# A table of pieces for units 2 to 13 of an attention and FFN kernel, and two three-operand weight passes on VectorE

## The chip, the cores and the metric

One NeuronCore of a Trainium2 chip runs the whole program in one launch. The metric is the device time in microseconds (us); a time stands for the median of several runs, and beside it stands one execution that the hardware profiler recorded.

## The reference

```python
# q, k, v: [4, 8, 576, 64]; w1: [1, 32]; b1: [32]; w2: [32, 8]
scores = (1/8) * q @ k.T                         # per batch and head
x = log1p(|i - j|) / log1p(max(i, 1))            # i, j: positions
bias = relu(x[..., None] @ w1 + b1) @ w2         # one 576x576 table per head
attn = softmax(scores + bias, over j)
y = attn @ v                                     # heads put side by side: [2304, 512]
h = y @ w_in                                     # w_in: [512, 2048], w_out: [2048, 512]
out = (h * cos(h)) @ w_out                       # float32
```

The inputs `moe_w_in` and `moe_w_out` come as 64-bit floats; the kernel reads them as pairs of 32-bit words and makes a high and a low float32r part of each itself.

## The kernel before

**Bias (0 to some 65 us).** 36 groups of rows of the bias tables are computed and stored to DRAM (`sc`), and read back as tiles `bt`.

**Attention (some 65 to 284 us).** The 16 units are pairs of heads of one batch. A unit has five slots, one for each tile of query rows; slot `j` has tile `tiles[j]` of `[0, 1, 4, 2, 3]`. Tiles 0 to 3 have 128 rows for each of two heads; tile 4 (slot 2) holds the last 64 rows of both heads, and counts as one head. For a tile the steps are, with short names that the text uses:

- S (`qk`, from the change on `scores`, L418): the scores, 12 matmuls (6 for tile 4) on TensorE into the PSUM tiles `s` (tag "s", two of them, two banks each). The array is used as two row tiles of 64x128, one per head; for tile 4 as one of 128x128.
- M (L431): VectorE adds the bias, keeps the row minimum of the negated sum, and frees `s`. One for each head.
- E (L449): ScalarE takes the exponential and the row sum. One for each head.
- D and R (L462, L465): VectorE adds 1e-9 to each head's sum and takes the reciprocal.
- N (L472): POOL multiplies the tile with it. One for each head.
- T (`halves`, L479): TensorE transposes the tile three slots later, in 64x128 row tiles, into the two PSUM banks `pm` (one buffer each). It also transposes pieces of neighbouring tiles into the bank `pt`.
- A and B (`keep_main`): ScalarE (A, L507) and VectorE (B, L510) copy the two halves of `pm` to `PT`, and so free `pm`. L (`keep_left`) copies `pt`.
- V (`pv`, L547): attn @ v for half `hf` (0: tiles 0, 1; 1: tiles 4, 2, 3), in five chunks of 128 keys, in column tiles of 128x64, into the one PSUM bank `pv`. One chunk is four matmul records. K (`keep_x`, L507 `xT`): ScalarE copies the finished half to `xT` and frees the bank.
- For the unit after next, q and k are transposed into a PSUM tile of tag "s" (F, `spare`), copied out by C (k: VectorE, q: ScalarE) and X (last rows), and split by POOL into high and low parts (P, `split`, L185 and L189).

**Weights.** A weight part is loaded as `raw`, made absolute by ScalarE ("abs", L93) and goes through four VectorE passes of 128x512 in `widen_w` (steps 0, 0.5, 1, 2: L101, L103, L105, L107; here W0, W0.5, W1, W2), a ScalarE copy (step 3) and a POOL subtraction (step 4, L111). Eight of the 32 parts are widened in the attention stage, one every two units, 24 in the FFN.

**FFN (some 284 us to the end).** 96 steps; each has 12 matmuls into `ph` (`ffn1`, L733), the cosine gate (L737, L743, L744, L748, L752, L756, L762), and 9 matmuls into `po` (`ffn2`, L779). `ph` has two buffers, and `gate` (L752, VectorE) frees one. POOL splits `xT` into `xs` (L532, L533), VectorE adds `po` up (L803).

**Order.** Every engine runs its instructions in the order in which the Python code issues them. In the attention stage `slot(i)` issues slot `i = 5u + j` by hand: S and M, then E of the last tile, T of the tile of three slots before, V, the copies, D, R, splits, N, loads, and the weight steps of `W_PLAN` and its kin. TensorE's order in a unit is thus

S0, T2, V(0: 0, 1), S1, V(0: 2, 3, 4), T3, F, S2, T4, S3, T0, V(1: 0, 1, 2), S4, T1, V(1: 3, 4)

with the number of the slot of the tile behind S and T, and half and chunks behind V.

Of the kernel before, what the change touches and what calls it, by code (L numbers as in the profile page):

```python
# [28 lines left out]
def kernel(  # L29
# [66 lines left out]
    def widen_w(fc, part, step=None):  # L96
        r, t, b = raw[fc, part], W[fc], wabs[fc, part]
        lo, hi = r[:, :, 0], r[:, :, 1]
        u = b.bitcast(U32)
        if step in (None, 0):  # L100
            nc.vector.tensor_scalar(b, b, 2.0**-15, None, ALU.max)  # L101
        if step in (None, 0.5):
            nc.vector.tensor_scalar(u, u, 3, 0x3FFFFFF8, ALU.logical_shift_left, ALU.bitwise_and)  # L103
        if step in (None, 1):
            nc.vector.scalar_tensor_tensor(u, lo, 29, u, ALU.logical_shift_right, ALU.bitwise_or)  # L105
        if step in (None, 2):
            nc.vector.scalar_tensor_tensor(u, hi, 0xC0000000, u, ALU.bitwise_and, ALU.bitwise_or)  # L107
        if step in (None, 3):
            nc.scalar.activation(out=t[:, 0, part], in_=b, func=AF.Copy)  # L109
        if step in (None, 4):  # L110
            nc.gpsimd.tensor_tensor(t[:, 1, part], b, f(t[:, 0, part]), ALU.subtract)  # L111

    with tc.manual_schedule():
# [82 lines left out]
        def natural(u, x):  # L196
            return nat[u, "k" if x == "x" else x].rearrange("p r h d -> p r (h d)")
# [13 lines left out]
            else:  # L211
                nc.scalar.activation(out=o, in_=i, func=AF.Copy, scale=-0.125)

        def keep_turned(u, x, ps):
            if x == "x":
                pq, pk_ = (ps[:, 0:64], ps[:, 64:128]) if not isinstance(ps, list) else ps
                o = kt.rearrange("p (a x) -> p a x", x=64)[:, 0:10:9]
                i = pk_.unsqueeze(1).to_broadcast([128, 2, 64])
                if u == 1:
# [6 lines left out]
                if u > 1:  # L226
# [179 lines left out]

        cur = {}

        def qk(u, j):
            t = tiles[j]  # L410
            heads = range(2 if t < 4 else 1)
            s = [ps_s.tile([128, 2, 512], F32, tag="s", name="s") for h in heads]
# [13 lines left out]
            hp = units[u][0]  # L426
            P[u, j] = pp.tile([128, 1152], F32, tag="p", name="P")
            for h in heads:
                neg = P[u, j][:, 576 * h : 576 * h + 576]
                m = sv.tile([128, 2], F32, tag=f"m{h}", name="m")  # L430
                nc.vector.tensor_tensor_reduce(  # L431
                    neg.rearrange("p (a x) -> p a x", a=2),
                    s[h][:, :, 0:HALF],
                    bias[hp, t, h].rearrange("p (a x) -> p a x", a=2),
                    1.0,
                    3.0e38,
                    ALU.add,
                    ALU.min,
                    m[:, 0:1],
                )  # L440
                cur[u, j, h] = (neg, m)

        P, dn, rc = {}, {}, {}

# [10 lines left out]
                accum_out=dn[u, j][:, h : h + 1],  # L455
            )

        def recip(u, j, step):
            n = 2 if tiles[j] < 4 else 1
            if step == 0:  # L460
                for h in range(n):
                    nc.vector.tensor_scalar(dn[u, j][:, h : h + 1], dn[u, j][:, h : h + 1], 1e-9, None, ALU.add)  # L462
            else:
                rc[u, j] = sv.tile([128, 2], F32, tag="rc", name="rc")
                nc.vector.reciprocal(rc[u, j][:, 0:n], dn[u, j][:, 0:n])  # L465
# [67 lines left out]
            nc.gpsimd.tensor_tensor(l, src, f(h), ALU.subtract)  # L533
            X[g, n, c] = (h, l)

        X_ = {}

        def pv(u, hf, chunks):
            hp, b = units[u]
            n = vN[u % 2]  # L540
# [15 lines left out]

        def keep_x(u, hf):
            hp, b = units[u]
# [13 lines left out]
        W_EARLY = [("abs", -1)]  # L572
        W_MID = [(3, 9)]
        W_PLAN = [(0, 2), (0.5, 3), (1, 7), (2, 8), ("load", 8), (4, 12)]
        get = lambda i: jobs[i] if 0 <= i < len(jobs) else None

        shared = {}
# [2 lines left out]
        def weights(i, plan):  # L580
            for step, at in plan:
                w, r = divmod(i - at, 10)
                if r == 0 and 0 <= w < len(wparts):
                    if step == "load":
                        if w + 2 < len(wparts):
                            load_w(*wparts[w + 2])
                    elif step == "abs":
                        abs_w(*wparts[w])
                    else:
                        widen_w(*wparts[w], step)  # L590

        def slot(i):
# [88 lines left out]
            if now and u == 0 and j == 0:  # L681
                split(1, "k")
            elif now and u == 0 and j == 1:
                split(1, "q")
            elif now:
                for du, x, step in POOL_PLAN[j]:
                    if u + du < NU and not (u == 0 and x == "q"):
# [6 lines left out]
            if now:  # L694
                if i == 1:
                    load(0, "v")
                for du, x in LOAD_PLAN[j]:
                    if u + du < NU:
# [232 lines left out]
```

## Time and profile before

| | |
|---|---|
| median of 3 runs | 699.49 us (697.37 to 701.4) |
| the profiled execution | 700.05 us |
| its span, first to last instruction | 698.3 us |
| mean granted TensorE clock | 0.995 of full speed |
| busy in the span: TensorE, VectorE, ScalarE, POOL | 98%, 83%, 62%, 58% |

Matmuls are pipelined and their ends are modelled, so two records overlap and a busy TensorE tells little: what counts is the distance from the start of one block of matmuls to the start of the next. In the rows below a line merges neighbouring instructions of one form; "PEld" are weight loads, "L431" is line 431 of the kernel.

### The profile page before, as it was taken

How to read it: one execution, taken by the hardware profiler on the slowest of the kernel's cores; microseconds unless marked ns; L12 is line 12 of the kernel's file. 1: busy time of each engine (PE TensorE's matmuls, PEld its weight loads, DVE VectorE, ACT ScalarE, POOL GpSimd, SP SyncE). 2: the span in 40 equal slices, each digit the busy share in tenths (PEclk: the TensorE clock that was granted, in tenths of full speed). 3: DMA queues.
4: the chain of work that ended last, by engine and by line, in shares of the span. 5: the costliest groups of instructions: out<-in, count | busy, mean ns of one | idle time of the engine just before them, and what ended most of it. 6: DMA issues, size and time to landing. Idle time of an engine off the chain costs nothing.

```text
span 698.3 us, 15617 instructions
## 1 busy us (share of the span) xinstructions
PE 683.7 (98%) x5747; PEld 564.9 (81%) x5747; DVE 581.1 (83%) x1342; ACT 434.9 (62%) x935; POOL 403.2 (58%) x486
## 2 busy tenths in 40 slices
PE   6998999999999999999999999999999999999997
PEld 3576777777777777788989999889989888999986
DVE  7997888888898888667887888999998998976666
ACT  5896888889888887645565554544545445433342
POOL 0306898988989899745454463563653744753300
PEclk9998999999999999999999999999999999999999
DMA  7798348238435501001121010111110111011112
GB/s 208 254 334 238 86 104 207 67 96 219 104 83 148 157 19 49 31 4 57 31 59 34 31 61 31 33 58 31 60 31 31 60 31 32 0 46 46 46 46 92
DMA packets 84446, 58.57 MB, mean 84 GB/s; under 512 B 62225, under 2 KB 70801, under 8 KB 84369
## 3 DMA queue, kind: packets, MB, share of 16 engines
q1 hardware_dynamic: 83024, 56.88, 28.2%
q8 instruction: 46, 0.75, 0.5%
q10 hardware_dynamic: 1344, 0.69, 0.4%
q14 instruction: 32, 0.25, 0.1%
HBM read 41.94 MB, written 15.61 MB: 82 GB/s over the span
## 4 chain that ended last, share of the span: by engine, by line
PE 94%; DVE 2%; DMA 1%; issue 1%; SPq 0%; ACT 0%; DVEq 0%; ACTq 0%
PE ph L733 29%; PE po L779 29%; PE pv L547 12%; PE s L418 11%; PE pm L479 6%; PE pa L332 5%; PE spare L479 1%; PE pt L479 1%; DVE P L431 1%; DVE ht L317 1%; DMA lt<-in_ltab_dram 1%; DMA bt<-sc 0%; DMA nk<-in_q_dram 0%; DVE acc L803 0%; DVE edge L302 0%
## 5 line engine op out<-in xcount | busy, mean ns | idle before, releaser
L431 DVE CUSTOM_DVE_ANT_0 P<-s,bt 128x576 f32<-128x576 f32 x144 | 103.7, 753 | 23.9 <-PE s L418 23.9
L472 POOL TENSOR_SCALAR P<-P,rc 128x576 f32<-128x576 f32 x144 | 107.7, 759 | 24.9 <-DVE rc L465 11.1
L737 ACT ACTIVATE a<-ph,quarter 128x384 int32<-128x384 f32 x96 | 55.6, 579 | 102.2 <-PE ph L733 101.2
L533 POOL TENSOR_TENSOR xs<-xT,xs 128x384 fp32r<-128x384 f32 x96 | 107.7, 1122 | 8.0
L449 ACT ACTIVATE P<-P,m 128x576 f32<-128x576 f32 x144 | 110.0, 768 | 1.0 <-POOL P L472 0.8
L733 PE MATMUL ph<-xs,wpre 128*128 128x384 f32 x576 | 109.4, 338 | 0.0
L733 PE MATMUL ph<-xs,w 128*128 128x384 f32 x576 | 108.3, 337 | 0.0
L743 DVE SCALAR_TENSOR_TENSOR r<-a,ph 128x384 f32<-128x384 int32 x96 | 52.8, 550 | 65.5 <-ACT a L737 65.3
L733 PEld LDWEIGHTS ph<-xs,wpre 128*128 128x128 f32 x576 | 101.8, 188 | 5.3 <-DVE a L752 0.9
L733 PEld LDWEIGHTS ph<-xs,w 128*128 128x128 f32 x576 | 101.5, 188 | 4.7 <-DVE a L752 0.6
L748 ACT ACTIVATE r<-r,hpi 128x384 f32<-128x384 f32 x96 | 59.3, 617 | 72.9 <-DVE r L744 72.7
L418 PE MATMUL s<-kN,qT 64*128 64x288 f32 (+1 forms) x864 | 93.8, 315 | 2.0 <-DVE m L431 1.5
L418 PEld LDWEIGHTS s<-kN,qT 64*128 64x128 f32 (+1 forms) x864 | 72.2, 188 | 27.1 <-DVE dn L462 8.5
L532 POOL TENSOR_SCALAR xs<-xT 128x384 fp32r<-128x384 f32 x96 | 62.7, 653 | 38.8 <-PE ph L733 38.8
L547 PE MATMUL pv<-PT,vN 128*64 128x320 f32 (+1 forms) x512 | 76.4, 420 | 0.0
L762 DVE TENSOR_TENSOR gl<-a,gh 128x384 fp32r<-128x384 f32 x96 | 74.4, 775 | 2.0 <-ACT gh L756 2.0
L779 PE MATMUL po<-wpre,gh 128*128 128x512 f32 x288 | 75.3, 397 | 0.0
L779 PE MATMUL po<-w,gh 128*128 128x512 f32 x288 | 75.2, 395 | 0.0
L111 POOL TENSOR_TENSOR w<-wb,w 128x512 fp32r<-128x512 f32 x16 | 20.7, 1296 | 89.3 <-ACT w L109 89.3
L744 DVE SCALAR_TENSOR_TENSOR r<-a,r 128x384 f32<-128x384 int32 x96 | 60.5, 630 | 3.3
L756 ACT ACTIVATE gh<-a 128x384 fp32r<-128x384 f32 x96 | 49.8, 519 | 21.2 <-DVE a L752 21.2
L779 PEld LDWEIGHTS po<-wpre,gh 128*128 128x128 f32 x288 | 53.4, 188 | 9.4 <-issue 0.5
(97 smaller groups left out, 1175.8 us busy)
## 6 DMA issues: line engine op xcount, KB each, us to landing
sc<-rt SPq DMA_DIRECT2D x36, 295.5 KB, 4.4
raw<-in_moe_w_in_dram SPq DMA_DIRECT2D x16, 512.0 KB, 3.8
raw<-in_moe_w_out_dram SPq DMA_DIRECT2D x16, 512.0 KB, 3.5
bt<-sc SPq DMA_DIRECT2D x16, 288.0 KB, 3.6
out_dram<-acc SPq DMA_DIRECT2D x17, 256.0 KB, 2.0
nk<-in_k_dram SPq DMA_DIRECT2D x32, 128.0 KB, 3.4
bt<-sc SPq DMA_DIRECT2D x16, 256.0 KB, 4.3
vN<-in_v_dram SPq DMA_DIRECT2D x32, 128.0 KB, 2.9
```

Source lines behind the costliest of these rows:

```text
L418: nc.tensor.matmul(s[h][:, hf, 0:HALF], qTs[u % 2][r, a, 128 * t : 128 * t + 128] if t < 4 else qTs[u % 2][:, a, 512:640], kN[u][r, b, o : ...
L431: nc.vector.tensor_tensor_reduce(neg.rearrange("p (a x) -> p a x", a=2), s[h][:, :, 0:HALF], bias[hp, t, h].rearrange("p (a x) -> p a x", ...
L449: nc.scalar.activation(out=P[u, j][:, 576 * h : 576 * h + 576], in_=neg, func=AF.Exp, bias=m[:, 0:1], scale=-1.0, accum_out=dn[u, j][:, h ...
L472: nc.gpsimd.tensor_scalar(p, p, r, 1.0, ALU.mult, ALU.mult)
L532: nc.gpsimd.tensor_scalar(h, src, 1.0, 1.0, ALU.mult, ALU.mult)
L533: nc.gpsimd.tensor_tensor(l, src, f(h), ALU.subtract)
L547: nc.tensor.matmul(ps[64 * h : 64 * h + 64, 0 : WQ[hf]], a, m, start=(c == 0), stop=(c == 4), tile_position=(0, 64 * h), skip_group_check= ...
L733: nc.tensor.matmul(ps, a, x, start=(i == 0), stop=(i == 3 * KD - 1))
L744: nc.vector.scalar_tensor_tensor(r, n, -TWO_PI_LO, r, ALU.mult, ALU.add)
L748: nc.scalar.activation(out=r, in_=r, func=AF.Sin, scale=SIN_SCALE, bias=hpi)
L762: nc.vector.tensor_tensor(gl, a, f(G[key][0]), ALU.subtract)
L779: nc.tensor.matmul(O[n][i], a[:, 128 * i : 128 * i + 128], w, start=(i0 == 0 and p == 0), stop=(i0 == GF - 1 and p == 2),)
```

## The change

`slot` no longer writes out slots 10 to 69 (units 2 to 13). They come from a table `PLAN` of five rows, one for each slot of a unit; an entry is a piece, its due slot counted from the start of the unit (or part of weights) that it belongs to, and its arguments. Units 0, 1, 14 and 15 keep the old order; `caught_up` issues, at the two borders, what one order has done and the other not. V's chunks are spread anew, so that TensorE's order in a unit is

S0, T2, V(0: 0, 3, 1), S1, T3, V(0: 2), F, S2, V(0: 4), T4, S3, T0, V(1: 0, 1, 2), S4, T1, V(1: 3, 4)

On VectorE the order of a unit is M0 (head 0), D4, M0 (head 1), X, R4, B2; M1, M1, D0, R0; B3, C, M2, D1, R1, B4; M3, M3, D2, R2, B0; M4 (head 0), D3, M4 (head 1), B1, R3. W1 stands first in slot 0 and W2 first in slot 3, of odd units (3, 5, ... 13), W0 last in slot 3 of odd units, W0.5 last in slot 2 of even units. On ScalarE, K of the second half stands behind both E of slot 4, no longer ahead of them. D takes its heads as an argument (both, in this table). Steps 0 and 0.5 of `widen_w`, in attention and FFN alike, become three-operand instructions: step 0 has its own input as second tensor, step 0.5 a constant column broadcast along the row.

```diff
+    field = const.tile([128, 1], F32, name="field")
@@ widen_w
         if step in (None, 0):
-            nc.vector.tensor_scalar(b, b, 2.0**-15, None, ALU.max)
+            nc.vector.scalar_tensor_tensor(b, b, 2.0**-15, b, ALU.max, ALU.max)
         if step in (None, 0.5):
-            nc.vector.tensor_scalar(u, u, 3, 0x3FFFFFF8, ALU.logical_shift_left, ALU.bitwise_and)
+            nc.vector.scalar_tensor_tensor(
+                u, u, 3, field[:, 0:1].bitcast(U32).to_broadcast([128, 512]), ALU.logical_shift_left, ALU.bitwise_and
+            )
...
+        nc.vector.memset(field, 2.0 - 2.0**-20)
...
-        def qk(u, j):
+        def scores(u, j):
...
+        def lowest(u, j, heads):
...
-        def recip(u, j, step):
+        def recip(u, j, step, heads=(0, 1)):
             n = 2 if tiles[j] < 4 else 1
             if step == 0:
-                for h in range(n):
+                for h in [h for h in heads if h < n]:
...
+        PLAN = [
+            [('W', 5, 1), ('E', 5, 4, 0), ('E', 5, 4, 1), ('S', 0), ('M', 0, 0, 0), ('D', 5, 4), ('K', 10, 1), ('T', 5, 2), ('M', 0, 0, 1), ('X', -10, 'k'), ('W', 10, 3), ('P', -5, 'q', 2), ('V', 5, 0, 0), ('X', -10, 'q'), ('LB', 0, 0), ('R', 5, 4), ('N', 5, 4, 0), ('V', 5, 0, 3), ('W', 10, 'load'), ('N', 5, 4, 1), ('L', 5, 0), ('W', 10, 4), ('A', 5, 2), ('B', 5, 2), ('V', 5, 0, 1)],
+            [('S', 1), ('W', -4, 'abs'), ('E', 1, 0, 0), ('E', 1, 0, 1), ('M', 1, 1, 0), ('M', 1, 1, 1), ('D', 1, 0), ('LB', 1, 1), ('R', 1, 0), ('N', 1, 0, 0), ('T', 6, 3), ('N', 1, 0, 1)],
+            [('A', 7, 3), ('B', 7, 3), ('V', 7, 0, 2), ('F', -8, 'k'), ('E', 2, 1, 0), ('E', 2, 1, 1), ('F', -8, 'q'), ('S', 2), ('C', -8, 'k'), ('P', -3, 'q', 1), ('M', 2, 2, 0), ('V', 7, 0, 4), ('LD', -13, 'q'), ('D', 2, 1), ('C', -8, 'q'), ('R', 2, 1), ('N', 2, 1, 0), ('K', 7, 0), ('N', 2, 1, 1), ('T', 7, 4), ('B', 7, 4), ('A', 7, 4), ('W', 2, 0.5), ('LB', 2, 2)],
+            [('S', 3), ('LD', -12, 'k'), ('E', 3, 2, 0), ('W', 8, 2), ('M', 3, 3, 0), ('T', 3, 0), ('M', 3, 3, 1), ('D', 3, 2), ('R', 3, 2), ('V', 8, 1, 0), ('B', 3, 0), ('N', 3, 2, 0), ('W', -2, 0), ('A', 3, 0), ('V', 8, 1, 1), ('LB', 3, 3), ('L', 8, 1), ('P', -7, 'k', 0)],
+            [('V', 9, 1, 2), ('E', 4, 3, 0), ('S', 4), ('M', 4, 4, 0), ('T', 4, 1), ('P', -6, 'q', 0), ('E', 4, 3, 1), ('D', 4, 3), ('P', -6, 'k', 1), ('A', 4, 1), ('V', 9, 1, 3), ('M', 4, 4, 1), ('V', 9, 1, 4), ('LD', -1, 'v'), ('B', 4, 1), ('LB', 4, 4), ('P', -6, 'k', 2), ('R', 4, 3), ('N', 4, 3, 1), ('N', 4, 3, 0)],
+        ]
...
+        def planned(i):
+            for op, f, *a in PLAN[i % 5]:
+                if op == "W":
+                    weights(i, [(a[0], f)])
+                elif 0 <= (i - f) // 5 < NU:
+                    step(op, (i - f) // 5, i, f, a)
+
+        FIRST, LAST = 10, 5 * (NU - 2)
...
         def slot(i):
             u, j = divmod(i, 5)
+            if i in (FIRST, LAST):
+                caught_up(i)
+            if FIRST <= i < LAST:
+                return planned(i)
```

## Rows read from the trace of the kernel before

**Rows 1.** The page: shares of the span, by engine, in the chain that ended last

```profile
PE 94%; DVE 2%; DMA 1%; issue 1%; SPq 0%; ACT 0%; DVEq 0%; ACTq 0%
```

**Rows 2.** Windows: one unit; length, then busy us of PE, PEld, DVE, ACT, POOL

```profile
178.77:193.06 14.29, 14.29 (x196) 10.63 (x195) 12.48 (x43) 11.73 (x32) 13.05 (x18) 1.00 0.38 85
```

**Rows 3.** Timeline, TensorE in one unit: start us, length us, what

```profile
183.37 1.05 PE L418 MATMUL s<-kN,qT 64*128 64x288 f32 x12
...
184.27 0.22 PE L479 MATMUL pm<-ident,nk 64*128 64x64 f32 x2
...
184.85 1.08 PE L547 MATMUL pv<-PT,vN 128*64 128x256 f32 x8
...
185.86 1.16 PE L418 MATMUL s<-kN,qT 64*128 64x288 f32 x12
...
186.95 1.08 PE L547 MATMUL pv<-PT,vN 128*64 128x256 f32 x8
...
187.87 0.60 PE L547 MATMUL pv<-PX,vN 128*64 128x256 f32 x4
...
188.40 0.71 PE L479 MATMUL pm<-ident,P 64*128 64x64 f32 x16
...
188.95 0.41 PE L479 MATMUL spare<-ident,nk 64*128 64x64 f32 x8
...
189.20 0.42 PE L479 MATMUL spare<-ident,nq 64*128 64x64 f32 x8
...
189.54 1.06 PE L418 MATMUL s<-kN,qT 128*128 128x288 f32 x6
...
190.53 0.65 PE L479 MATMUL pm<-ident,P 64*128 64x64 f32 x14
...
191.18 1.33 PE L418 MATMUL s<-kN,qT 64*128 64x288 f32 x12
...
192.23 0.77 PE L479 MATMUL pm<-ident,P 64*128 64x64 f32 x16
...
193.06 1.30 PE L547 MATMUL pv<-PT,vN 128*64 128x320 f32 x8
```

**Rows 4.** Timeline of the same unit: ScalarE, VectorE and POOL, with idle time before

```profile
183.51 0.44 ACT L507 ACTIVATE xT<-pv 128x320 f32<-128x320 f32 x1 [0.67 <-PE pv L547]
...
183.72 0.88 POOL L189 TENSOR_TENSOR kN<-kt,kN 128x320 fp32r<-128x320 f32 x1
183.85 0.77 ACT L449 ACTIVATE P<-P,m 128x576 f32<-128x576 f32 x1
...
184.46 0.76 DVE L431 CUSTOM_DVE_ANT_0 P<-s,bt 128x576 f32<-128x576 f32 x1 [0.59 <-PE s L418]
...
185.15 0.75 DVE L431 CUSTOM_DVE_ANT_0 P<-s,bt 128x576 f32<-128x576 f32 x1
...
191.45 0.68 DVE L510 COPY PT<-pm 128x512 f32<-128x512 f32 x1
```

**Rows 5.** By line: three weight passes; least, median and longest ns of one

```profile
L101 DVE TENSOR_SCALAR wb<-wb x32: 404/728/1232, 62.0 to 595.0; 128x512 f32<-128x512 f32 x32
...
L103 DVE TENSOR_SCALAR wb<-wb x32: 426/1114/1179, 65.0 to 595.8; 128x512 uint32<-128x512 uint32 x32
...
L105 DVE SCALAR_TENSOR_TENSOR wb<-raw,wb x32: 669/684/1506, 77.7 to 599.5; 128x512 uint32<-128x512 uint32 x32
```

**Rows 6.** Timeline, FFN stage: weight passes, and what stands beside and behind them

```profile
346.58 1.20 POOL L533 TENSOR_TENSOR xs<-xT,xs 128x384 fp32r<-128x384 f32 x1
346.83 1.50 DVE L105 SCALAR_TENSOR_TENSOR wb<-raw,wb 128x512 uint32<-128x512 uint32 x1
...
457.27 1.12 DVE L103 TENSOR_SCALAR wb<-wb 128x512 uint32<-128x512 uint32 x1
458.31 0.54 DVE L752 TENSOR_TENSOR a<-r,ph 128x384 f32<-128x384 f32 x1
...
458.91 2.37 PE L733 MATMUL ph<-xs,w 128*128 128x384 f32 x12
```

More of the change, by code (lines that the diff above doesn't have):

```diff
@@ L212, in keep_pair, with keep_turned @@
                 nc.scalar.activation(out=o, in_=i, func=AF.Copy, scale=-0.125)
-        def keep_turned(u, x, ps):
+        def keep_turned(u, x, ps, part=None):
             if x == "x":
@@ L218, in keep_turned @@
                 i = pk_.unsqueeze(1).to_broadcast([128, 2, 64])
+                if part == "k":
+                    nc.vector.tensor_copy(o, i)
+                    return
                 if u == 1:
@@ L225, in keep_turned @@
                     )
-                if u > 1:
+                if u > 1 and part is None:
                     nc.vector.tensor_copy(o, i)
@@ L407, with scores_of_rest, scores_of_rest_begun @@
         cur = {}
-        def qk(u, j):
+        def scores_of_rest(u, s, step):
+            for n, (a, b) in enumerate(((0, 0), (0, 1), (1, 0))):
+                for h in range(2):
+                    r, hf = slice(64 * h, 64 * h + 64), h ^ step
+                    o = HALF * hf + 64
+                    nc.tensor.matmul(
+                        s[:, hf, 0:HALF],
+                        qTs[u % 2][r, a, 512:640],
+                        kN[u][r, b, o : o + HALF],
+                        start=(step == 0 and n == 0),
+                        stop=(step == 1 and n == 2),
+                        tile_position=(r.start, 0),
+                    )
+        live = {}
+        def scores_of_rest_begun(u):
+            live[u, 2] = [ps_s.tile([128, 2, 512], F32, tag="s", name="s")]
+            scores_of_rest(u, live[u, 2][0], 0)
+            nc.sync.keepalive_nop(ins=[nc.sync.lower_ap(live[u, 2][0][:, :, 0:HALF])])
+        def scores(u, j):
             t = tiles[j]
             heads = range(2 if t < 4 else 1)
-            s = [ps_s.tile([128, 2, 512], F32, tag="s", name="s") for h in heads]
+            if (u, j) in live:
+                scores_of_rest(u, live[u, j][0], 1)
+                return
+            s = live[u, j] = [ps_s.tile([128, 2, 512], F32, tag="s", name="s") for h in heads]
             for hf in range(2):
@@ L425, in qk @@
                         )
-            hp = units[u][0]
-            P[u, j] = pp.tile([128, 1152], F32, tag="p", name="P")
+        def lowest(u, j, heads):
+            t, s, hp = tiles[j], live[u, j], units[u][0]
+            if (u, j) not in P:
+                P[u, j] = pp.tile([128, 1152], F32, tag="p", name="P")
             for h in heads:
@@ L441, in qk @@
                 cur[u, j, h] = (neg, m)
+        def qk(u, j):
+            scores(u, j)
+            lowest(u, j, range(2 if tiles[j] < 4 else 1))
         P, dn, rc = {}, {}, {}
@@ L534, in split_x, with once @@
             X[g, n, c] = (h, l)
-        X_ = {}
+        X_, ran = {}, set()
+        def once(*what):
+            new = what not in ran
+            ran.add(what)
+            return new
         def pv(u, hf, chunks):
             hp, b = units[u]
+            chunks = [c for c in chunks if once("V", u, hf, c)]
             n = vN[u % 2]
@@ L557, in keep_x @@
         def keep_x(u, hf):
+            if not once("K", u, hf):
+                return
             hp, b = units[u]
@@ L582, in weights @@
                 w, r = divmod(i - at, 10)
-                if r == 0 and 0 <= w < len(wparts):
+                if r == 0 and 0 <= w < len(wparts) and once("W", w, step):
                     if step == "load":
@@ L590, in weights, with turn_spare, step @@
                         widen_w(*wparts[w], step)
+        def turn_spare(u, x, spare):
+            at = 256 * "kq".index(x)
+            for c in range(4):
+                for r in range(2):
+                    flip(spare[:, r, at + 64 * c : at + 64 * c + 64], natural(u, x)[:, c], r)
+        PM, left = {}, {}
+        def step(op, u, i, f, a):
+            j = f % 5
+            if op == "S":
+                scores(u, f)
+            elif op == "Sa":
+                scores_of_rest_begun(u)
+            elif op == "M":
+                lowest(u, a[0], a[1:])
+            elif op == "E":
+                softmax_exp(u, *a)
+            elif op == "D":
+                recip(u, a[0], 0, a[1:] or (0, 1))
+            elif op == "R":
+                recip(u, a[0], 1)
+            elif op == "N":
+                norm(u, *a)
+            elif op == "T":
+                p = a[0]
+                if p in (0, 2):
+                    alloc_half(u, p // 2)
+                ahead, behind, both = [], [], None
+                if p in (1, 4):
+                    src = [P[u, p - 1][:, 512:640], P[u, p][:, 512:640]]
+                    shared[0] = bank(), src, (u, 0 if p == 1 else 1)
+                    ahead = [(shared[0][0][:, 128 * n : 128 * n + 64], x) for n, x in enumerate(src)]
+                elif p in (0, 2) and 0 in shared:
+                    gone = shared.pop(0)
+                    behind = [(gone[0][:, 128 * n + 64 : 128 * n + 128], x) for n, x in enumerate(gone[1])]
+                    left[gone[2]] = gone[0]
+                if p == 2 and 2 <= u + 3 < NU:
+                    both = u + 3
+                PM[u, p] = halves((u, p), ahead, behind, both)
+            elif op == "A":
+                keep_main(u, a[0], 0, PM[u, a[0]][0])
+            elif op == "B":
+                keep_main(u, a[0], 1, PM[u, a[0]][1])
+            elif op == "X":
+                keep_turned(u, "x", [PM[u - 3, 2][r][:, 320:384] for r in range(2)], a[0])
+            elif op == "L":
+                keep_left(u, a[0], left[u, a[0]][:, 0:256])
+            elif op == "V":
+                pv(u, a[0], a[1:])
+            elif op == "K":
+                keep_x(u, a[0])
+            elif op == "F":
+                if ("spare", u) not in shared:
+                    shared["spare", u] = ps_s.tile([128, 2, 512], F32, tag="s", name="spare")
+                turn_spare(u, a[0], shared["spare", u])
+            elif op == "C":
+                at = 256 * "kq".index(a[0])
+                keep_pair(u, a[0], shared["spare", u][:, :, at : at + 256])
+            elif op == "P":
+                if once("P", u, *a):
+                    split(u, *a)
+            elif op == "LD":
+                if once("LD", u, *a):
+                    load(u, a[0])
+            elif op == "LB":
+                hp, b = units[u]
+                if b == B - 1 and hp + 1 < HP:
+                    load_bias(hp + 1, tiles[a[0]])
@@ new lines, in planned, with caught_up @@
+        def planned(i):
[5 more added lines that the diff above has]
+        FIRST, LAST = 10, 5 * (NU - 2)
+        def caught_up(i):
+            for ops in PLAN:
+                for op, f, *a in ops:
+                    if op == "W":
+                        for w in range(len(wparts)):
+                            at, before = 10 * w + f, 10 * w + LEGACY[(op, a[0])]
+                            if min(at, before) < i <= max(at, before):
+                                weights(at, [(a[0], f)])
+                    elif (op, *a) in LEGACY:
+                        for u in range(NU):
+                            at, before = 5 * u + f, 5 * u + LEGACY[(op, *a)]
+                            if min(at, before) < i <= max(at, before):
+                                step(op, u, i, f, a)
@@ L686, in slot @@
                 for du, x, step in POOL_PLAN[j]:
-                    if u + du < NU and not (u == 0 and x == "q"):
+                    if u + du < NU and not (u == 0 and x == "q") and once("P", u + du, x, step):
                         split(u + du, x, step)
@@ L697, in slot @@
                 for du, x in LOAD_PLAN[j]:
-                    if u + du < NU:
+                    if u + du < NU and once("LD", u + du, x):
                         load(u + du, x)
```

2 lines of the change are left out of this document (added), and 6 rows, old and new, of the table LEGACY.

## The prediction

> **What bounds the kernel now.** I read the chain of waits first: 94% of it is TensorE [rows 1], so a change pays only where TensorE starts a block late, and VectorE, ScalarE or POOL count only where they make it late. Then the window of one unit: 14.29 us, in which TensorE's records cover everything, VectorE has 12.48 and POOL 13.05 us of work [rows 2]. Covered is not full, since ends are modelled, so I measured blocks from start to start [rows 3]. Two kinds of lost time show.
>
> *Changes of the array's shape.* Eight pv matmuls take 0.92 us where pv goes on (186.95 to 187.87) and 1.01 where scores follow (184.85 to 185.86): leaving pv costs 0.09. Four of them and the exit take 0.53 (187.87 to 188.40), so a matmul is 0.11 and entering pv costs 0.92 - 0.88 = 0.04. Eight transposes take 0.25 before more transposes and 0.34 before the 128x128 scores (188.95, 189.20, 189.54): leaving 0.09; sixteen take 0.55 behind pv (188.40 to 188.95), so entering is 0.05. Scores followed by transposes, both 64x128, pay nothing: 0.90 us (183.37 to 184.27). All [rows 3].
>
> *Waits.* S1 takes 1.09 (185.86 to 186.95) against 0.90 + 0.09: 0.10 lost, because its second head waits for M0, begun at 185.15 [rows 3, 4]. S3 starts at 191.18, right behind T4, but T0 follows only at 192.23, 1.05 later; with 0.90 less an entry of some 0.10 it would be 0.80, so 0.25 are lost to M2. T0 takes 0.83 (to 193.06) against T4's 0.65 (190.53 to 191.18) less 0.05 entry plus 0.09 exit, 0.69: its two halves ran askew, 0.14 lost [rows 3].
>
> In all 0.49 us a unit can be had, 5.9 us in the 12 units of the table.
>
> **The change part by part.** The work of TensorE is the same.
>
> *Visits to pv.* Before, four: S1-V-T3 and S2-T4 are among the borders. After, five: T3-V-F and S2-V-T4. The first replaces S1-V-T3 at the same price; the second puts a visit where only S2-T4 (0.14) stood, at 0.13 + 0.14. Added: 0.13 us a unit, 1.6 us in 12.
>
> The rule of the Trainium skill that speaks against the change is that a change of tiling mode, not only of the tile, drains TensorE (page "TensorEngine Tiling (Array Packing)", Key Properties). The trace agrees: the same pv matmuls end 0.09 us later where the shape changes [rows 3]. Without the rule this term would be 0 and the sum 1.6 us lower.
>
> *S1's wait.* M0's second head now stands behind two additions of D4, some 0.13 us, but S1 comes 0.43 later (four more pv matmuls). Counted from S0's start, M0 begins at 1.09 (183.37 to 184.46) and the second head ends at 1.09 + 0.69 + 0.13 + 0.75 = 2.66; S1 is due at 0.90 + 0.58 + 1.01 + 0.43 = 2.92 [rows 3, 4]. The wait goes: -0.10 a unit, -1.2 us.
>
> *S3's wait, and what is late next.* V(0: 4) between S2 and T4 gives M2 time, so S3 need not wait. But T0 writes the banks that B4 empties, and B4 begins once T4 ends: B4 runs 191.45 to 192.13, T0 starts 0.10 later already now [rows 3, 4]. T4 to B4 to T0 stays, so the 0.25 of S3 becomes a wait of T0. Only the skew goes, 0.14, less some 0.05 for weights loaded after a wait: -0.09 a unit, -1.1 us. If B4 were no bound it would be -4 us.
>
> *K behind two exponentials.* V(0: 0) of slot 0 needs the bank that K frees. Now ScalarE idles 0.67 us for it (from 182.84), runs K, then E (183.85). After: two E at 0.77 from 182.84, then K 0.44, end at 184.82; V(0: 0) is due at 183.37 + 1.48 = 184.85 [rows 3, 4]. Nothing is lost, but the room is 0.03 us. I take 0; ends 0 and 0.3 a unit (a rival).
>
> *W passes in attention.* A two-tensor pass waits while POOL is within an instruction: L105 takes 0.67 us free and 1.50 when L533 had 0.95 left; 0.95 - 0.13 + 0.68 = 1.50 [rows 5, 6]. L101 and L103 take 0.40 and 0.43 free and wait the same way (1.12 in [rows 6]). So the three-operand form doesn't evade POOL, and lasts 0.26 and 0.24 longer. W1 now stands in slot 0 of six odd units in VectorE's gap of 0.59 before M0 [rows 4]; it fills it, and any wait for POOL goes to M0, whose room before S1 is 0.26. POOL is then in a run of P and N (0.88 one P [rows 4]; busy 13.05 of 14.29 [rows 2]). A wait lies between 0 and 0.75, so the cost between 0 and 0.5 a time; I take 0.25, near the middle of a P: +1.5 us in six (0 to 3). W0, W0.5 and W2 lie ahead of M4 and M3 in gaps: 0, up to 1.5 without that cover. POOL itself is delayed by as much, and N is used over a microsecond later: 0.
>
> *The FFN.* Each of 24 parts keeps VectorE 0.50 us longer. What hides that is the time between the end of L752, which frees `ph`, and the matmuls into it. At 458.85 and 458.91 it is 0.06, and so it is at the two like places 50 and 101 us later; elsewhere I find 0.6 or more. Three times 0.45: +1.3 us (0 to 3).
>
> The Trainium skill says of this that a VectorE instruction in a two-port mode or with two SBUF inputs and a POOL instruction exclude one another for a whole instruction (page "SBUF — State Buffer", section "SBUF: two separate sides"). The rows agree to 0.13 us. Were only the means compared (L103 is long, L105 mostly short), the FFN term would be about -0.8 instead of +1.3.
>
> *Other.* Splits and loads move by a slot or less; q's first split waits for S4 on POOL, with over a slot until its use: 0. The border slots 10 and 70: 0 ± 0.5.
>
> Sum: 1.6 - 1.2 - 1.1 + 1.5 + 1.3 = +2.1 on the profiled 700.05, 702.1. That execution lies 0.56 above the median of 699.49; taken off, **701.6 us**. About 0.5% (3.5 us) is what a measurement can tell from no change; this is within.
>
> **The rivals.**
> - *K late (slower).* Decides once E starts over 0.03 us later than worked out. By 0.3 in each of 12 units it gives 3.6 us more, 705.2. For: all of M4, D3, A1 stand before E, and D3 now stands between the two M4. Against: ScalarE has idle time before T1. Chance 0.25.
> - *Three-operand passes don't wait.* Then L101 and L103 are 0.67 each in the FFN, the waits there go (-0.8), the rest stays: 699.5. Against it L105's 1.50. Chance 0.15.
> - *B4 is no bound.* T0 follows S3 at 0.80, and W1 meets no POOL instruction: -3.0 - 1.5, so 697.1, and 695.0 if the FFN's passes don't wait either. Against: [rows 4]. Chance 0.15.
> - *Nothing shows:* the order's gains and W1's cost cancel, the FFN hides its passes: 699.5, chance 0.10.
>
> **How the numbers follow.** The forecast has 0.35, with its own range 699 to 704; part of it, and of K late, lies over 703, so slower by over 0.5% has 0.30. Faster by over 0.5% (under 696) is most of the case in which B4 is no bound: 0.12. Within: 0.58. For 8 in 10 I take 696.5 to 706.
>
> **What would show it.** Right: units of 14.2 us without W1 and 14.4 with it; S1 at 0.90 to the next block in even units, late in odd ones; T0 1.7 us after T4's start as now; L101 and L103 at some 0.98 and 1.36 us where L532 and L533 run, and `ph` some 0.5 us late at three places. Wrong: V(0: 0) late after K; S3 or S0 still waiting for M; passes that don't wait for POOL; units under 14.

## The result, and the profile after

The changed kernel takes 706.47 us (median of 6 runs, 703.19 to 708.80) against 700.12 for the kernel before (6 runs beside it): ratio 1.0095, with a 95% interval of 1.0071 to 1.012, 0.95% slower. The forecast was 701.6 with a range up to 706.0. The profiled execution took 707.25 us, its span is 705.5; before they were 700.05 and 698.3, so the span has 7.2 us to account for.

The page of the changed kernel; the chain that ended last, by engine (compare [rows 1]):

```profile
PE 64%; DVE 25%; issue 5%; ACT 3%; DMA 2%; POOL 1%; SPq 0%; DVEq 0%; ACTq 0%; POOLq 0%
```

VectorE had 2% of the chain before and has 25% now. Windows of the changed kernel; length, then busy us of PE, PEld, DVE, ACT and POOL, and the granted clock (first the stretch from one S2 to the next around the first unit, then one steady unit, then two stretches of the FFN):

```profile
59.12:76.04 16.92, 14.36 (x158) 10.92 (x156) 13.01 (x45) 11.98 (x33) 15.61 (x21) 0.80 0.61 143
...
190.10:204.28 14.18, 14.18 (x199) 10.36 (x195) 12.82 (x43) 12.46 (x33) 12.69 (x18) 1.00 0.38 97
300.00:450.00 150.00, 149.11 (x746) 133.27 (x745) 127.85 (x191) 79.12 (x145) 82.16 (x82) 1.00 0.13 39
450.00:600.00 150.00, 146.80 (x725) 129.44 (x725) 138.65 (x212) 71.59 (x129) 77.84 (x79) 1.00 0.12 39
```

The same stretches of the kernel before:

```profile
59.16:75.15 15.99, 14.19 (x158) 11.26 (x156) 12.56 (x45) 11.97 (x33) 14.57 (x21) 0.79 0.64 152
300.00:450.00 150.00, 150.00 (x751) 135.37 (x751) 122.68 (x194) 80.22 (x147) 78.05 (x83) 1.00 0.13 39
450.00:600.00 150.00, 150.00 (x750) 134.64 (x749) 137.03 (x218) 72.76 (x131) 79.34 (x84) 1.00 0.12 39
```

A steady unit is 0.11 shorter than before (14.29 in [rows 2]); in the FFN TensorE, which had no gap, now has gaps.

I put every number of the attention stage on one ruler, the starts of S2 in units 0 to 15. From unit 0 to 1 the distance is 15.99 before and 16.92 after. From unit 1 to 14 it is 185.24 before (75.15 to 260.39) and 185.25 after (76.04 to 261.29). Unit 15's S2 starts at 274.05 and 274.93. So up to there the changed kernel is 0.9 us behind, all of it from the first unit, and the other 6.3 us lie behind it. One thing must be known of that first unit: in some of the traces TensorE runs part of it at the lower clock level and in others not (the granted clock in the window is 0.80 and 0.79 above, and 1.00 in the run of the new order alone, where the distance is 14.17). Where it does, the distance lies between 15.99 and 17.56, and it is 16.91 in a run below whose attention stage is that of the kernel before (the same move in the kernel before). The 0.9 us are therefore not put down to the change.

For the FFN I use one measure throughout: the distances from the start of one block of matmuls (12 into `ph` or 9 into `po`) to the next, 186 of them from the first `po` block on. An undisturbed one is some 2.105 us; what is above that, added up, is called the FFN's excess. Before it is 0.99 us, after 7.64. The +6.65 is the loss by this measure; with the distances under 2.105 counted against it, it is 6.2, which fits the 6.3 above.

The weight passes by line, after; least, median and longest ns of one:

```profile
L102 DVE SCALAR_TENSOR_TENSOR wb<-wb x32: 670/986/1502, 61.9 to 602.1; 128x512 f32<-128x512 f32 x32
L104 DVE SCALAR_TENSOR_TENSOR wb<-wb,field x32: 699/1389/1449, 65.2 to 603.1; 128x512 uint32<-128x512 uint32 x32
```

Against [rows 5] (0.728 and 1.114) they are 0.26 and 0.27 us longer, forecast 0.26 and 0.24. Where it hurts, the timeline of the changed kernel shows (start us, length us; idle time before in brackets). VectorE:

```profile
454.39 0.68 DVE L110 SCALAR_TENSOR_TENSOR wb<-raw,wb 128x512 uint32<-128x512 uint32 x1
454.99 0.55 DVE L910 TENSOR_TENSOR a<-r,ph 128x384 f32<-128x384 f32 x1
455.45 0.68 DVE L961 TENSOR_TENSOR acc<-acc,po 128x512 f32<-128x512 f32 x1
456.80 0.55 DVE L901 SCALAR_TENSOR_TENSOR r<-a,ph 128x384 f32<-128x384 int32 x1 [0.67 <-ACT a L895]
...
457.92 1.37 DVE L920 TENSOR_TENSOR gl<-a,gh 128x384 fp32r<-128x384 f32 x1
459.22 0.98 DVE L102 SCALAR_TENSOR_TENSOR wb<-wb 128x512 f32<-128x512 f32 x1
460.24 1.39 DVE L104 SCALAR_TENSOR_TENSOR wb<-wb,field 128x512 uint32<-128x512 uint32 x1
461.55 0.54 DVE L910 TENSOR_TENSOR a<-r,ph 128x384 f32<-128x384 f32 x1
```

ScalarE beside it:

```profile
455.11 0.64 ACT L112 ACTIVATE wpre<-wb 128x512 fp32r<-128x512 f32 x1 [0.45 <-DVE wb L110]
455.64 0.65 ACT L94 ACTIVATE wb<-raw 128x512 f32<-128x512 f32 x1
456.20 0.57 ACT L895 ACTIVATE a<-ph,quarter 128x384 int32<-128x384 f32 x1
```

And TensorE:

```profile
456.81 2.25 PE L891 MATMUL ph<-xs,w 128*128 128x384 f32 x12
458.90 1.56 PE L937 MATMUL po<-w,gh 128*128 128x512 f32 x6
460.29 0.86 PE L937 MATMUL po<-w,gl 128*128 128x512 f32 x3
462.14 2.36 PE L891 MATMUL ph<-xs,w 128*128 128x384 f32 x12 [0.99 <-DVE a L910]
```

TensorE waits 0.99 us for L910, and from 454.39 to 462.09 VectorE has one idle time, 0.67 us at 456.80. The same place before (the gate and `ph` that follow are [rows 6]); VectorE:

```profile
451.69 0.69 DVE L107 SCALAR_TENSOR_TENSOR wb<-raw,wb 128x512 uint32<-128x512 uint32 x1
...
454.10 0.56 DVE L743 SCALAR_TENSOR_TENSOR r<-a,ph 128x384 f32<-128x384 int32 x1 [0.67 <-ACT a L737]
...
456.51 0.73 DVE L101 TENSOR_SCALAR wb<-wb 128x512 f32<-128x512 f32 x1
```

and TensorE:

```profile
454.62 2.27 PE L733 MATMUL ph<-xs,w 128*128 128x384 f32 x12
```

Set the two against TensorE's `ph` block of that step: L743 started 0.52 us ahead of it (454.10 and 454.62), L901 starts with it (456.80 and 456.81). VectorE comes into this part 0.51 later against TensorE than before, needs 0.54 more for it (456.80 to 462.09 is 5.29; 454.10 to 458.85 was 4.75), and had 0.06 of room: 0.51 + 0.54 - 0.06 = 0.99. And its idle time is 0.67 in both, although it is late in one: that idle time is not a reserve.

### The profile page after: what moved, and what is told of

It reads as the page before. It is cut to its first block, busy times and chain, and to the rows that moved or that the text cites. A ratio compares the mean times of both kernels' runs of the same rounds, so it can differ in the third digit from the quotient of the medians.

```text
span 705.5 us, 15651 instructions
## 1 busy us (share of the span) xinstructions
PE 685.6 (97%) x5747; PEld 559.8 (79%) x5747; DVE 600.8 (85%) x1343; ACT 435.5 (62%) x935; POOL 420.4 (60%) x486
## 4 chain that ended last, share of the span: by engine, by line
PE 64%; DVE 25%; issue 5%; ACT 3%; DMA 2%; POOL 1%; SPq 0%; DVEq 0%; ACTq 0%; POOLq 0%
PE ph L891 17%; PE po L937 15%; PE pv L591 11%; PE s L449 10%; PE pm L517 5%; PE pa L339 5%; DVE gl L920 5%; DVE wb L104 3%; DVE r L901 3%; DVE wb L102 2%; DVE acc L961 2%; DVE a L910 2%; DVE wb L108 2%; DVE P L465 2%; DVE wb L110 1%
## 5 line engine op out<-in xcount | busy, mean ns | idle before, releaser
L465 DVE CUSTOM_DVE_ANT_0 P<-s,bt 128x576 f32<-128x576 f32 x144 | 105.3, 751 | 21.9 <-PE s L449 21.5
L510 POOL TENSOR_SCALAR P<-P,rc 128x576 f32<-128x576 f32 x144 | 114.3, 805 | 9.4 <-DVE rc L503 2.8
L571 POOL TENSOR_TENSOR xs<-xT,xs 128x384 fp32r<-128x384 f32 x96 | 112.4, 1171 | 8.0
L901 DVE SCALAR_TENSOR_TENSOR r<-a,ph 128x384 f32<-128x384 int32 x96 | 52.7, 549 | 58.0 <-ACT a L895 57.9
L449 PE MATMUL s<-kN,qT 64*128 64x288 f32 (+1 forms) x864 | 90.8, 314 | 2.8 <-DVE m L465 1.7
L449 PEld LDWEIGHTS s<-kN,qT 64*128 64x128 f32 (+1 forms) x864 | 70.6, 189 | 27.3 <-DVE m L465 10.7
L570 POOL TENSOR_SCALAR xs<-xT 128x384 fp32r<-128x384 f32 x96 | 67.6, 704 | 37.2 <-PE ph L891 37.2
```

The lines of the kernel that those rows point to most:

```text
L449: nc.tensor.matmul(s[h][:, hf, 0:HALF], qTs[u % 2][r, a, 128 * t : 128 * t + 128] if t < 4 else qTs[u % 2][:, a, 512:640], kN[u][r, b, o : ...
L465: nc.vector.tensor_tensor_reduce(neg.rearrange("p (a x) -> p a x", a=2), s[h][:, :, 0:HALF], bias[hp, t, h].rearrange("p (a x) -> p a x", ...
L510: nc.gpsimd.tensor_scalar(p, p, r, 1.0, ALU.mult, ALU.mult)
L570: nc.gpsimd.tensor_scalar(h, src, 1.0, 1.0, ALU.mult, ALU.mult)
L901: nc.vector.scalar_tensor_tensor(r, n, -TWO_PI_HI, ps, ALU.mult, ALU.add)
```

## The experiments

Ratios are to the kernel before on the same chip and have their 95% interval. The first four runs stand beside 697.93 us of it, the next three beside 700.57.

**The order alone.** The whole table, with the two weight passes as before.

```diff
-            nc.vector.scalar_tensor_tensor(b, b, 2.0**-15, b, ALU.max, ALU.max)
+            nc.vector.tensor_scalar(b, b, 2.0**-15, None, ALU.max)
@@ and step 0.5 likewise, back to tensor_scalar
```

> The changed order, with the two weight passes as two-operand passes again. Theory (the FFN pays for the longer passes of VectorE): the stretch from the last 128x288 scores to the end, 430.6 us in the changed kernel and 424.3 in the one before, goes back to 424.3, and the whole is 699.5 to 701 us. Rival (the new order hands the FFN over in another phase, and the passes cost little): the stretch stays near 430 and the whole near 706.

699.59 us, ratio 1.0004 (0.9981 to 1.0027); FFN's excess 1.01. The order moves the whole by nothing that can be measured (the medians lie 0.24% apart, within the interval), and the FFN is back. Units without W1 take 14.14 to 14.22 but for one of 14.47, five of the six with it 14.32 to 14.52. One of the latter, VectorE:

```profile
153.24 1.26 DVE L105 SCALAR_TENSOR_TENSOR wb<-raw,wb 128x512 uint32<-128x512 uint32 x1
154.43 0.74 DVE L461 CUSTOM_DVE_ANT_0 P<-s,bt 128x576 f32<-128x576 f32 x1
```

and POOL:

```profile
152.25 1.71 POOL L189 TENSOR_TENSOR kN<-kt,kN 128x320 fp32r<-128x320 f32 x2
153.93 1.92 POOL L506 TENSOR_SCALAR P<-P,rc 128x576 f32<-128x576 f32 x2
```

W1 (L105) starts within POOL's second L189, lasts 1.26 in place of 0.68, and M0 starts at its end.

**The passes alone.** The old order, both passes three-operand throughout.

```diff
@@ widen_w of the kernel before
-            nc.vector.tensor_scalar(b, b, 2.0**-15, None, ALU.max)
+            nc.vector.scalar_tensor_tensor(b, b, 2.0**-15, b, ALU.max, ALU.max)
@@ and step 0.5 likewise, as in the change
```

> The old order, with both passes in three-operand form everywhere. Theory: the FFN stretch is 430 to 431 us, and the first units lose some 0.9 us beside it: 706.5 to 707.5 us. Rival (the order is the cause): 700 to 701.5 us.

707.42, ratio 1.0134 (1.0111 to 1.0158); excess 7.82, units 14.29 as before. The passes alone make the whole loss. That the ratio is above the changed kernel's 1.0095 goes with the clock: all four executions have a mean granted clock of 0.992 to 0.994, while 10 of the 19 beside them of the kernel before have 1.000.

**The passes in the FFN alone.**

```diff
+            if fc >= WPRE:
+                nc.vector.scalar_tensor_tensor(b, b, 2.0**-15, b, ALU.max, ALU.max)
+            else:
+                nc.vector.tensor_scalar(b, b, 2.0**-15, None, ALU.max)
@@ and step 0.5 likewise
```

> The old order; both passes in three-operand form for the 24 weight parts of the FFN, in the old form for the eight of the attention stage. Theory: 6.0 to 6.5 us more than before, all of it behind the attention stage, and attention as before to 0.2 us. If the 0.9 us of the first units come from the pass in attention, they are gone here; if they come from something else, they stay.

704.04, ratio 1.0098 (1.0066 to 1.0129); excess 7.71. It is the 24 parts of the FFN. This is the base of the runs that follow.

**The first pass in the FFN alone.** As the last, with step 0.5 as before, so that each part is 0.26 us longer instead of 0.5.

```diff
@@ step 0.5
+            nc.vector.tensor_scalar(u, u, 3, 0x3FFFFFF8, ALU.logical_shift_left, ALU.bitwise_and)
```

> The old order; in the FFN only the first of the two passes (the maximum) in three-operand form, so that VectorE is kept some 0.26 us longer for a part, not 0.51. If what VectorE loses is carried from one part to the next over twelve FFN steps (three parts) until a stall of TensorE clears it: 3 x 0.26 less the room of 0.06 at three places, some 0.7 us each, and 0.1 to 0.2 at two more, so 2.4 us, 702.5. If every part stands for itself, as the prediction had it: 3 x 0.2 = 0.6 us, 700.7.

700.64, ratio 1.0037 (1.0017 to 1.0057); excess 3.03. At the three places where before had 0.06 of room the loss is 0.75, 0.74 and 0.53 us, up to three times what one part adds. So a part's 0.26 doesn't stay in that part: it is carried to the next. The first of the three places, TensorE:

```profile
454.61 1.56 PE L782 MATMUL po<-w,gh 128*128 128x512 f32 x6
456.01 0.86 PE L782 MATMUL po<-w,gl 128*128 128x512 f32 x3
457.46 2.37 PE L736 MATMUL ph<-xs,w 128*128 128x384 f32 x12 [0.59 <-DVE a L755]
```

(From 454.61 to 457.46 is 2.85, 0.75 over 2.105. The expectation took three parts for 12 steps; a part takes three steps, so there are four.)

**ScalarE's copy and abs later, with the longer passes.** My theory was that the 0.67 of idle time ahead of L743 is lost cover: VectorE waits for `a`, which stands on ScalarE behind the copy of VectorE's own last pass and behind the next abs. So both were put behind the next step's `a`.

```diff
+        late = []
@@ widen_step: steps 3 and 4 and load_next; begin_widen: abs_w
-                widen_w(*p, step)
+                late.append(lambda step=step: widen_w(*p, step))
...
@@ ffn_step
                 ffn1(now)
+            while late:
+                late.pop(0)()
```

> The old order in attention, three-operand passes in the FFN alone, and on ScalarE the weight copy (step 3) and the absolute value of the next part put behind the next step's first activation (the one that reads ph) instead of ahead of it. Theory (what VectorE loses is never made good, because once a part it sits idle 0.66 us for an activation that stands on ScalarE behind two weight instructions, which wait for VectorE's own last pass): the idle time goes, and with it up to 0.66 of the lag a part; the phases of the FFN's matmuls over 2.105 us add up to 2 to 3 us, not 7.6, and the whole is some 4 to 5 us under the run with three-operand passes in the FFN alone. Rival (VectorE has too much work, whatever waits where): they stay near 7 us.

716.11, ratio 1.0234 (1.0198 to 1.0269); excess 16.57 against 7.71, a loss in place of a gain. VectorE in this run:

```profile
447.81 0.56 DVE L753 SCALAR_TENSOR_TENSOR r<-a,ph 128x384 f32<-128x384 int32 x1 [0.33 <-ACT a L747]
448.40 1.70 DVE L754 SCALAR_TENSOR_TENSOR r<-a,r 128x384 f32<-128x384 int32 x1
450.02 0.85 DVE L772 TENSOR_TENSOR gl<-a,gh 128x384 fp32r<-128x384 f32 x1
450.80 1.50 DVE L103 SCALAR_TENSOR_TENSOR wb<-wb 128x512 f32<-128x512 f32 x1
```

and POOL:

```profile
448.38 1.30 POOL L120 TENSOR_TENSOR wpre<-wb,wpre 128x512 fp32r<-128x512 f32 x1 [7.48 <-ACT wpre L118]
```

The idle time did shrink, to 0.33. But POOL's subtraction (L120) waits for the copy and moved with it. It began 0.02 us ahead of L754, which needs 0.56 alone and took 1.70: 448.38 + 1.30 - 0.14 + 0.56 = 450.10, its end. In the unmoved order (the run of the FFN passes alone) the subtraction ran from 452.00 to 453.30, across the idle time and L753 (452.98, 0.55), which reads PSUM and isn't held up, and L754 came behind it.

**The same move in the kernel before.**

```diff
@@ the late list of the last run, two-operand passes
```

> The kernel before, with that move on ScalarE alone. Theory: the small waits at three places of the FFN (0.9 to 1.0 us in all) shrink to 0.5 us or less; attention as before. Rival: nothing changes, or the later copy makes a weight part late and the waits grow.

704.62 (one run), excess 4.40 against 0.99. The move is bad by itself, by the same collision: L744 takes 1.69 at 443.08, beside a subtraction that begins at 443.06.

**W1 moved, with that move.** The order alone, ('W', 5, 1) of the first row of the table as ('W', 3, 1) at the end of its fourth row, and the late list.

```diff
-            [('W', 5, 1), ('E', 5, 4, 0), ('E', 5, 4, 1), ('S', 0), ...
+            [('E', 5, 4, 0), ('E', 5, 4, 1), ('S', 0), ...
...
-             ..., ('LB', 3, 3), ('L', 8, 1), ('P', -7, 'k', 0)],
+             ..., ('LB', 3, 3), ('L', 8, 1), ('P', -7, 'k', 0), ('W', 3, 1)],
@@ and the late list
```

> The changed order with two-operand passes, W1 put from the head of slot 0 of odd units to the end of slot 3 of even ones, and the move on ScalarE. Theory (W1 at the head of slot 0 waits for POOL and makes the slot's blocks late): every unit of the table takes 14.19 us, where the order alone had 14.3 to 14.5 in odd ones; 12 x 0.1 in attention and some 0.5 in the FFN less than before, 697.9 - 1.7 = 696.2. Rival (another wait takes W1's place, in slot 4): units stay at 14.3 on the mean, and the whole within 0.1% of before.

703.09, ratio 1.0036 (1.0016 to 1.0056). The FFN has the 4.40 of the last run. In the attention stage the units are 14.19 to 14.22 but for one of 14.78, and units 1 to 14 take 184.85 us, 0.4 less than before.

**W1 moved alone.** The same without the late list.

> The order of the change with two-operand weight passes, and the plan's entry for the third weight pass (W1) moved from the first place of unit slot 5 to the last place of slot 3, nothing else. Theory (in the order-alone kernel the odd units are 14.32 to 14.52 us because W1 on VectorE waits there for GpSimd, L105 1.05 to 1.26 us, and all others are 14.18): steady units are 14.18 to 14.22 throughout as in the run that moved ScalarE's copies too, the thirteen units from the second S2 to the fourteenth take 184.9 us instead of 185.4, and the FFN's excess over 2.105 us per phase stays at the 0.9 of the order-alone kernel, so the kernel is 0.5 us below the kernel before. Rival (the odd units take their time from the order itself): 185.4 us again, the same as before.

699.75 (before 700.28), ratio 0.9997 (0.9977 to 1.0017); excess 1.00. Steady units 14.18 to 14.22, so W1's wait is what the odd units had more. But units 1 to 14 took 186.24, not 184.9: one unit took 15.73, for which the waits of TensorE give this (engine, line, waited for; us in total, times, longest):

```profile
PE pm L513 <- DMA nk<-in_q_dram: 1.2, 1, 1.2
```

and another 14.59. The transposes of the last q and k rows (tile `nk`), which open T2, had to wait for their load; in the run before it was 0.35 us, once. The 15.73 stands at the same place as the odd distance of the run before, from unit 3's S2 to unit 4's. T2 comes late there in every kernel with the new order (that distance is 14.52 in the changed one, 14.47 with the order alone, 14.78, 15.73 here, 14.89 in the last run) and in none with the old (14.28 to 14.30). In three of the five the profile puts it down to that load. So a late T2 at this place belongs to the new order; why the load is late was not tried.

**The longer passes without the sums.** The FFN-passes-alone kernel without VectorE's additions of `po` in the second and third of four groups of 24 steps; it leaves those sums out of its output.

```diff
@@ drain
+            if not final:
+                return
```

> The FFN-passes-alone kernel with VectorE's additions of po to acc left out in the second and third of the four groups of 24 steps (the output lacks those two groups' sums; no other work is removed). Theory of the carried lag (the two longer passes put VectorE 0.51 us behind per weight part, and the lag is carried over the part's end because the wait of L753 for ScalarE's a is itself set by VectorE's last weight pass, through the weight copy and the next abs; additions of 0.68 us outside of that wait are what leaves no room): both groups come out like the first group of that kernel, which has no such additions, one stall of about 0.5 us per 12 steps instead of 1.5, so the FFN's excess falls from 7.6 to about 3.5. Rival (each part's own step with both longer passes is late, whatever else VectorE does): the excess stays at 6 to 7.6.

699.91 (one run; before 700.28), excess 3.50 where 3.5 was expected: one stall of 0.5 to 0.7 per 12 steps in all groups, where the second and third group had 1.5. VectorE here:

```profile
451.02 0.55 DVE L762 TENSOR_TENSOR a<-r,ph 128x384 f32<-128x384 f32 x1
452.83 0.56 DVE L753 SCALAR_TENSOR_TENSOR r<-a,ph 128x384 f32<-128x384 int32 x1 [1.26 <-ACT a L747]
```

The addition that stood between these two is gone, and the wait is 1.26 instead of 0.66: that one was worth nothing, since the wait ends by ScalarE's `a` all the same. So the 4.2 us must come from the additions outside of it; they were not taken out apart from this one.

**The two passes in two steps.**

```diff
-... for s in ((0, 0.5), (1,), (2, 3, 4)))
+... for s in ((0,), (0.5, 1), (2, 3, 4)))
```

> The FFN-passes-alone kernel with the second weight pass moved from the step of the first to the step of the third, so that no step holds both longer passes. Theory of the carried lag (what counts is VectorE's sum over the steps of one part, between two waits that its own last pass sets): the FFN's excess stays near 7.6, 6 to 9 us, with the late phase one step further on. Rival (the one step that holds both passes is too full, by 0.5): the excess falls to 1 to 3 us.

702.42 (one run; before 700.28), excess 6.06: at the lower end of the 6 to 9 of the carried lag and far from 1 to 3. At the three places one wait of 1.4 us stands one step later (463.0, 515.0, 566.8); most of the small ones of 0.1 to 0.3 went. Spreading the work recovers 1.6 of the 6.7 us that the passes add to the excess; what matters more is the sum over the part.

**The abs alone later.** The FFN-passes-alone kernel with only the abs in the late list; copy and subtraction where they were.

```diff
@@ begin_widen
-            abs_w(*p)
+            late.append(lambda: abs_w(*p))
```

> The FFN-passes-alone kernel with only ScalarE's next abs put behind the next step's a; the weight copy (L118) and GpSimd's subtraction behind it (L120) stay where they were. In the FFN-passes-alone kernel VectorE's one idle time per part is 0.66 us, ahead of L753, which waits for a behind the copy and the abs (0.53 us of issue each). If that wait is the lost cover, a comes 0.53 us earlier, about the 0.51 us that the longer passes cost per part, and the FFN's excess falls from 7.6 to 1 to 3 us. The run with both moved got worse, where GpSimd's subtraction came later and stood across VectorE's next passes (L754 1.70 us in place of 0.56). If VectorE's progress after the wait is set by GpSimd's chain (subtraction at 452.00, splits behind it), which isn't moved here, an earlier a only turns into a longer wait of L754 or L772, and the excess stays at 6 to 8.

702.41 (one run, granted clock 0.993; before 701.48, one run); excess 2.71, within 1 to 3. ScalarE:

```profile
453.10 0.63 ACT L118 ACTIVATE wpre<-wb 128x512 fp32r<-128x512 f32 x1 [0.46 <-DVE wb L116]
453.64 0.57 ACT L747 ACTIVATE a<-ph,quarter 128x384 int32<-128x384 f32 x1
454.11 0.66 ACT L94 ACTIVATE wb<-raw 128x512 f32<-128x512 f32 x1
```

and POOL:

```profile
453.81 1.30 POOL L120 TENSOR_TENSOR wpre<-wb,wpre 128x512 fp32r<-128x512 f32 x1 [3.06 <-ACT wpre L118]
```

`a` starts 0.54 behind the copy's start in place of 1.09 (455.11 to 456.20 after), and the subtraction stays right behind the copy. That one edit gives back 5.0 of the 6.7 us, with the two passes together as long as without it (2.37 us, by the part that begins at 455.41 there and at 456.23 here). So the first theory of the idle time was right, and what spoiled it was the copy with its subtraction that moved along.

**A version for both.** W1 moved and the abs later, with two-operand passes.

> The order of the change with two-operand passes, W1 at the end of slot 3 (as in the run before the last ones), and ScalarE's next abs put behind the next step's a, as in the run that gave 4.9 us of the FFN's excess back. Theory: VectorE's room of about 0.5 us per part grows, so the excess of 0.9 to 1.0 us that is left in the FFN with two-operand passes goes to 0 to 0.5, with the attention's units at 14.18 to 14.22: 0.5 to 1.5 us below the kernel before, ratio 0.998 to 0.999. Rival (with the shorter passes the earlier a makes VectorE's next passes meet GpSimd's subtraction, as in the run with both copies moved, where the excess was 4.4): the excess rises to 2 to 4 and the kernel is not faster than before.

699.81 (before 700.22), ratio 0.9994 (0.9974 to 1.0014). The excess fell from 1.0 to 0.65, a little less than hoped; one of the three places still waits. The units are 14.18 to 14.22, as expected, but for one of 14.89 and one of 14.30. The kernel can't be told apart from the one before, and the 0.5 to 1.5 us that were expected are not shown; by the two ratios it is about 1% below the changed one.

## Why the prediction was wrong

The sum was +2.1 us; the profiled execution lies 7.2 higher: 0.9 in the first unit, 0.0 from unit 1 to 14, where the sum had +0.8, and 6.3 behind it, where the sum had +1.3. By its terms:

- **Visits to pv, right.** The changed kernel's TensorE in one unit (rows that open a block, as [rows 3] for before):

```profile
190.10 1.05 PE L449 MATMUL s<-kN,qT 128*128 128x288 f32 x6
191.09 0.65 PE L591 MATMUL pv<-PX,vN 128*64 128x256 f32 x4
191.67 0.65 PE L517 MATMUL pm<-ident,P 64*128 64x64 f32 x14
...
193.28 0.71 PE L517 MATMUL pm<-ident,P 64*128 64x64 f32 x16
...
201.57 1.06 PE L449 MATMUL s<-kN,qT 64*128 64x288 f32 x12
202.47 0.65 PE L517 MATMUL pm<-ident,P 64*128 64x64 f32 x16
203.05 0.65 PE L591 MATMUL pv<-PT,vN 128*64 128x256 f32 x4
203.63 0.46 PE L517 MATMUL spare<-ident,nk 64*128 64x64 f32 x8
```

  A visit of four pv matmuls takes 0.58 (191.09 to 191.67, 203.05 to 203.63); four at 0.11 and the 0.13 of entry and exit are 0.57.
- **S1's wait, right.** 0.90 to T3 (201.57 to 202.47), as forecast; 1.09 before.
- **S3 and T0, right in kind.** T0 starts 1.61 behind T4 (191.67 to 193.28), 1.70 before, 1.7 forecast; it is still bound behind B4, which runs from 192.42 for 0.69. The gain is 0.15 a unit in place of 0.09, which makes a steady unit 14.18 instead of 14.2; over half of it is T0's earlier start, which the prediction had at nothing, and the skew went only in part (T0 takes 0.76, to 194.04, against 0.83).
- **K late: didn't happen.** T2 takes 0.58 (199.54 to 200.12), with no wait of V(0: 0).
- **W1's wait for POOL, right as a mechanism, too dear.** Forecast +0.25 in six units. In the order-alone kernel it is 0.14 to 0.33 in most of them. In the changed kernel it costs 0.52 in one (L108 1.43 at 127.62; that unit takes 14.70) and nothing in the others, where W1 lasts 0.68 to 0.94: up to 0.27 more than its 0.67, which M0's room of 0.26 takes. With +0.4 at the two borders (forecast 0 ± 0.5) and 0.33 of one late T2, units 1 to 14 come out at +0.0. That they cancel is luck: neither the late T2 nor a W1 that costs in one unit of six was foreseen.
- **The FFN, the step that failed.** "Three times 0.45: +1.3 us (0 to 3)" measured +6.65. The price of a pass was right to 0.03 us, and so was the reading that a three-operand pass waits for POOL as a two-tensor pass does. Wrong was what hides it. I took the room ahead of each `ph` (0.06 at three places, "elsewhere I find 0.6 or more") as new for every part, so that 0.45 vanish wherever the room is 0.6. That holds only if VectorE is back on time when the next part begins. It isn't: four parts fall on 12 steps, VectorE's one idle time in a part is the wait for `a`, and `a` stands on ScalarE behind the copy of VectorE's last pass, so a late VectorE gets a late `a` and the same 0.67 of idle time. Per 12 steps 4 × 0.53 us are added, and from the second group of 24 steps on 1.5 come out as stalls, at three parts of the four. The runs bear this out from three sides: half the added time gives 0.75 where a single part adds 0.26; less work of VectorE brings the excess from 7.71 to 3.50; `a` taken out from behind the abs brings it to 2.71.

The upper bound was wrong too. With 24 parts at 0.50 the bound for no cover at all was 12 us, and the profile had the reason to use it: VectorE was 83% busy over the span, and 91% (137.03 of 150) in the second stretch above. The rival that was slower (K late) was not the one that came. That the passes don't wait for POOL is refuted by L102 and L104 above, and that B4 is no bound by T0.

The Trainium skill states that a VectorE instruction with two SBUF inputs and a POOL instruction that reads SBUF shut one another out for a whole instruction (page "SBUF — State Buffer", section "SBUF: two separate sides"). The trace agrees, with 1.70 us for L754 beside a subtraction and 0.56 alone.

## What to carry to other kernels

Room ahead of a wait counts once for a run of steps, not once for each step, unless an idle time between them really lets the engine catch up; ask of each idle time what ends it, and if that is something that the engine itself started, it moves along and is no reserve. Add up what a change puts on such an engine over the whole period and take no cover as the upper bound. And where two engines shut each other out, moving one instruction moves the others that wait for it: choose the move that leaves the other engine's instructions where they were.

## What the runs showed of the hardware

- A VectorE instruction that reads two SBUF operands and begins while a POOL instruction runs lasted until 0.14 us before that one's end plus its own length: 1.70 in place of 0.56 (448.40 above), and 1.26 in place of 0.68 (153.24 above, beside the second L189, which ends at 153.96). L901, which reads PSUM, takes its 0.55 at 456.80 although a subtraction runs from 455.82 to 457.12:

```profile
455.82 1.30 POOL L114 TENSOR_TENSOR wpre<-wb,wpre 128x512 fp32r<-128x512 f32 x1 [4.48 <-ACT wpre L112]
```

  I had counted this for the weight passes, and not for the gate's own instructions.
- The granted clock of the first unit goes with 2 to 3 us of an execution: 0.79 with 15.99 us, 0.80 with 16.92, and 1.00 with 14.17 in the order-alone run. In the changed kernel the clock is at 0.50, the level of 1.2 GHz, from 67 to 73 us, behind waits of TensorE for VectorE of 1.04 and 0.28 us at 63.96 and 64.64. In the order-alone run waits of 0.76, 0.28, 0.26 and 0.28 stand there and the clock doesn't fall; in the kernel before 0.77 and 0.28 stand there and it falls. What decides it stays open. So does whether the longer passes ahead of the FFN have a part in it: of the ten executions with them (six of the changed kernel, four of the passes alone) one has a mean granted clock of 0.999 or more, and of 70 of the kernel before on four chips 29 have it.
